# Ramp, turns and hand-over of a fused linear attention and top-1 expert kernel in a new order, and two steps of the first expert's second products over all its columns

## The chip, the cores and the metric

One core of one Trainium2 chip runs one program. The metric is the time of one execution on the device in microseconds, median of three runs. TensorE multiplies, VectorE and GpSimd (POOL in the profile) work element by element, ScalarE evaluates functions and copies, SyncE (SP) issues DMAs. Each engine works through its own instructions in order and waits for the others at semaphores.

## The reference

```
f = sigmoid(f_logit)                         # q, k, v, f_logit: [4, 8, 768, 48]
for t in range(768):                         # per batch and head
    state = f[t, :, None] * state + outer(k[t], v[t])
    y[t] = q[t] @ state
x = y.transpose(0, 2, 1, 3).reshape(3072, 384)
logits = x @ w_gate                          # 8 experts
e = argmax(logits, 1); gate = softmax(logits)[e]
out = gate * sigmoid(x @ w_output_gate)[e] * (relu(x @ w1[e]) @ w2[e])   # w1 384x1024, w2 1024x384
```

Everything is float32. The expert products are made from three matmuls of fp32r pieces each: high by high, low by high, high by low.

## The kernel before, in words

**Attention.** The sequence is cut in chunks of 128 positions, six per batch, 24 in all; a step t is one chunk of one batch, all 8 heads. Within a chunk the gates are turned into running products: ScalarE writes f (L214) into a PSUM bank, VectorE scans it twice, p (L219) and its inverse i (L226), POOL multiplies q by p (L234) and k by i (L231), in place. TensorE then makes the scores a_ps (`qk`, L256), a mask is put on them (half by POOL after a copy, L261 and L262, half by VectorE, `at`, L265), k is transposed (`kn_tr`, L275), and y of the chunk is the sum of a product with the state (`out_state`, L319) and one with the masked scores (`out_at`, L327), in two PSUM banks, two_ps and one_ps. The state is renewed from a product (L292) and two VectorE instructions (L306, L307; one, L304, for the first chunk of a batch). ScalarE copies y out of both banks (`evac_y`, L341), TensorE transposes it and multiplies it by the gate weights (`x_tr`, L350), VectorE finds each token's expert (`route`, L404 to L410) and its slot by a rank product (L433, L435, L441, L443), and POOL scatters the rows by an indirect DMA to a buffer sorted by expert (L369).

**What sets the order.** Nothing is scheduled: the order in which `attention` calls the steps is the order of each engine's instructions. The steps are pipelined: f is made two steps ahead, the scores and y of the previous step stand in one turn of the loop, y is transposed a step later. The first steps fill this pipeline (the ramp, steps 0 to 2). A change of batch, at steps 6, 12 and 18, is called a turn here: there y's sum starts without a state. At the last step, 23, `hand_over` takes the place of the loop's end: it mixes the last two chunks with the start of the experts.

**Experts.** They come in order of their number of tokens, with 448, 432, 416, 400, 400, 384, 368 and 368 columns. F = 1024 is cut in 8 blocks f. `mm1` (L862) makes 9 matmuls per f into h_ps, ScalarE's relu gives the high part (`hh`, L866), VectorE the low one (`hl`, L867); `mm2` (L882, and L896 for later experts) adds 9 matmuls per f to y_ps. Weights are split likewise, the high part on ScalarE (L695), the low part on VectorE or POOL (L696, `w1l`, `w2l`). The first expert starts while the last tokens are still being scattered: its first 224 columns (EARLY) go through mm1 for all f (`mm1_early`) and through mm2 for the first AHEAD = 8 of them; then the late columns are fetched (`x_late`, L812 and L819), and they go through mm1 and mm2. VectorE finds the other tokens' lists in between (`find_order`, L943 to L960).

Of the kernel before, what the change touches and what calls it, by code (L numbers as in the profile page):

```python
# [8 lines left out]
F32 = mybir.dt.float32  # L9
F32R = mybir.dt.float32r  # L10
# [23 lines left out]
HARD = 64  # L34
T_TOP = 16
T_END = 20
AHEAD = 8
KC = DM // 128
KF = F // 128
BIG = 8192  # L40
# [25 lines left out]
def make_consts(nc, k, pool, prep, ps, ends):  # L66

    k.warm = pool.tile([128, 512], BF16, name="warm")
    nc.vector.memset(k.warm, 0.0)
    warm_up(nc, k, ps, WARM)  # L70
    k.act = pool.tile([128, 1], F32, name="act")
    nc.scalar.activation(out=k.act, in_=k.warm[:, 0:1], func=AF.Sigmoid)

    for a in ends:
        nc.vector.memset(a, 0.0)

    k.start_p = [prep.tile([128, NP, C], F32, name=f"start_p{i}", bufs=1) for i in range(2)]
    for t in k.start_p:
        nc.vector.memset(t, PFLOOR)

    k.start_i = [prep.tile([128, NP, C], F32, name=f"start_i{i}", bufs=1) for i in range(2)]
    for t in k.start_i:
        nc.vector.memset(t, 0.0)
    k.ident = pool.tile([128, 128], F32, name="ident")
    make_identity(nc, k.ident)

    k.mask = pool.tile([128, NP, C], F32, name="mask")
    nc.gpsimd.memset(k.mask, 1.0)
    nc.gpsimd.affine_select(out=k.mask, in_=k.mask, pattern=[[0, NP], [1, C]], compare_op=ALU.is_ge,
                            fill=0.0, base=0, channel_multiplier=-1)  # L90


# [42 lines left out]
def attention(ctx, tc, nc, k, kpool, rt, q01, k01, f01, q23, k23, f23, v, wg, xs_dram, r, ex):  # L135
# [61 lines left out]
    def prep(ti):  # L197
        b, c = order[ti]
        i, sl, z = b % 2, slice(c * C, (c + 1) * C), ti % 2
        flat = lambda a: a.rearrange("p g t -> p (g t)")  # L200
        eng = nc.vector if ti == last else nc.gpsimd
        kcuts = [slice(0, 2), slice(2, NP)] if ti in (1, 2) else [slice(0, NP)]
        d = {}

        def s():

            nc.scalar.activation(out=k.start_p[z][:, :, 0:1], in_=f_t[i][:, :, c * C:c * C + 1], func=AF.Sigmoid)  # L207
            d["p"] = pf.tile([128, NP, C], F32, name="p", bufs=3)
            nc.scalar.copy(out=d["p"][:, 0, 0:1], in_=k.start_p[z][:, 0, 0:1])

        def f():

            d["f"] = {1: f_y, 2: f_o, 4: f_m}.get(ti, f_ps)
            nc.scalar.activation(out=d["f"][:, :, 0:C - 1], in_=f_t[i][:, :, c * C + 1:c * C + C], func=AF.Sigmoid)  # L214

        def scan_p():

            n, sp = NP * C, flat(k.start_p[z])
            nc.vector.tensor_tensor_scan(out=flat(d["p"])[:, 1:n], data0=flat(d["f"])[:, 0:n - 1], data1=sp[:, 1:n],  # L219
                                         initial=sp[:, 0:1], op0=ALU.mult, op1=ALU.max)  # L220

        def scan_i():

            nc.vector.reciprocal(out=k.start_i[z][:, :, C - 1:C], in_=d["p"][:, :, C - 1:C])
            d["i"] = pf.tile([128, NP, C], F32, name="i", bufs=3)
            nc.vector.tensor_tensor_scan(out=flat(d["i"])[:, ::-1], data0=flat(d["f"])[:, ::-1],  # L226
                                         data1=flat(k.start_i[z])[:, ::-1], initial=0.0, op0=ALU.mult, op1=ALU.max)

        def mul_k():
            for h in kcuts:  # L230
                eng.tensor_tensor(out=k_t[i][:, h, sl], in0=k_t[i][:, h, sl], in1=d["i"][:, h], op=ALU.mult)  # L231

# [11 lines left out]
    def hot(t):  # L244
        return 0 <= t < len(order)
# [200 lines left out]
    def hand_over():  # L446
        even, odd = (0, 1, 4, 5), (2, 3, 6, 7)
        run_pq()
        evac_y(last - 1, (0,))
        state_upd(last - 1)  # L450
        evac_y(last - 1, (1,))
        ex.x_early_turn()
        y_at(last)
        out_at(last, even, True)
        out_at(last, odd, True)
        scatter(4)
        x_tr(last - 1)
        ex.x_early()
        for heads in (even, odd):
            out_state(last, heads, False)  # L460
        evac_x(last - 1)
        evac_y(last)
        ex.split(1, 0, 1)
        ex.mm1_early(0)
        x_tr(last)
        evac_x(last)
        route(len(RG) - 1, last - 1, 2)
        drain()
        ex.split(1, 0, 2)
        ex.mm1_early(1)  # L470
        ex.split(1, 0, 3, nc.gpsimd)
        ex.mm1_early(2)
        run_pq()
        scatter(len(sq))
        ex.tokens_in(0, FIRST // TS, NT)
        ex.meta_in(0)

# [18 lines left out]

    done = [set() for _ in order]
    f_y, f_m = pairs(two), pairs(misc)
    f_o = pairs(one)
    make_consts(nc, k, kpool, pf, psA.tile([128, 2, 512], F32, name="kx")[:, 0, :],  # L500
                [a[:, :, C - 1:C] for a in (f_ps, f_y, f_o, f_m)])
    for st in states:
        nc.gpsimd.memset(st, 0.0)
    for g in range(2):
# [19 lines left out]
    for t in range(last + 1):  # L524
# [26 lines left out]
        fill(more)  # L551
        kn_tr(t)
        if t == 0:
            warm_up(nc, k, misc, 3)
        if t == last:
            run_pq(ready)
        if hot(t - 2):
            x_tr(t - 2)
        evac_kn(t)
# [5 lines left out]
        if t == last:  # L565
            route(*ends[t - 2])
            drain()
        fill(more)
        if T_END <= t < last:
            fill(8)  # L570
# [4 lines left out]
            psX.append(ctx.enter_context(tc.tile_pool(name="psX", bufs=1, space=PSUM)))  # L575
        if hot(t - 1):
            out_y(t - 1)
            if order[t - 1][1] < NCH - 1 and t < last and not ready:
                evac_y(t - 1, (0,))
                halved.append(t - 1)  # L580
            state(t - 1)
# [1 line left out]
            hand_over()  # L583
            break
        run_pq(ready)
        if t >= T_END:
            pre(t + 2, "mul_k")
        if t >= T_SCAT:
            scatter(1 if t < T_END else 2)
# [18 lines left out]
        if t + 1 == last:  # L608
            drain()
            assert ex.xq  # L610
            ex.split(1, 0, 0)
    for f in range(3, KF):
        ex.mm1_early(f)
        if f == 3:
# [6 lines left out]
class Experts:  # L621
# [4 lines left out]
    def __init__(self, tc, nc, k, r, raw, right, w1, w2, xs_dram, out, kp):  # L626
        self.tc, self.nc, self.k, self.r, self.raw, self.right, self.kp = tc, nc, k, r, raw, right, kp
        self.w1, self.w2, self.xs, self.out = w1, w2, xs_dram.rearrange("(e n) w -> e n w", e=E), out

        self.first = kp.tile([128, SLOTS // BL, QW], F32, name="first_x")  # L630
        self.apart, self.number, self.meta, self.put_out = [], {}, {}, []
        self.cleared = {HELD // TS: []}
        self.wr, self.whl, self.todo, self.gq = {}, {}, [], []
        self.xq, self.xt, self.hs, self.ysb = {}, {}, {}, {}

    def open_early(self):
# [47 lines left out]
            self.wr[2, s, i] = t  # L684

    def split(self, m, s, i, eng=None):
        to = of = lambda a: a.rearrange("p a b -> p (a b)")
        if m == 2 and s < TURNED:
            to = lambda a: a.rearrange("p a b -> p (a b)").rearrange("p (c x i) -> p x c i", c=KC, i=BL)
            of = lambda a: a.rearrange("p a (q c i) -> p (a q) c i", c=KC, i=BL)  # L690
        t = self.wr.pop((m, s, i))
        shape = [128, KC, 256] if m == 1 else [128, 2, DM]
        hi = self.wp.tile(shape, F32R, name=f"w{m}h")
        lo = self.wp.tile(shape, F32R, name=f"w{m}l")
        self.nc.scalar.copy(out=to(hi), in_=of(t))  # L695
        (eng or self.nc.vector).tensor_tensor(out=to(lo), in0=of(t), in1=to(hi.bitcast(F32)), op=ALU.subtract)  # L696
        self.whl[m, s, i] = (hi, lo)


    def rows(self, s):  # L700
        return [(j, min(TS, CAPS[s] - j * TS)) for j in range(NT) if CAPS[s] > j * TS]
# [149 lines left out]
    def mm1(self, s, f, early=False):  # L851
# [6 lines left out]
        for c in range(KC):  # L858
            cs = slice((f % 2) * 128, (f % 2) * 128 + 128)
            xh, xl = self.xt[x, c]  # L860
            for a, b in ((wh, xh), (wh, xl), (wl, xh)):
                nc.tensor.matmul(ps[:, 0:n], a[:, c, cs], b, start=(i == 0), stop=(i == 3 * KC - 1))  # L862
                i += 1
        pool, width = (self.ha, EARLY) if early else (self.hp, WIDE)
        hi, lo = (pool.tile([128, width], F32R, name=m)[:, 0:n] for m in ("hh", "hl"))
        nc.scalar.activation(out=hi, in_=ps[:, 0:n], func=AF.Relu)  # L866
        nc.vector.scalar_tensor_tensor(out=lo, in0=ps[:, 0:n], scalar=0.0, in1=hi.bitcast(F32), op0=ALU.max,  # L867
                                       op1=ALU.subtract)
        self.hs.setdefault((s, f), []).append((hi, lo))
# [450 lines left out]
```

## Time and profile before

| | us |
|---|---|
| median of 3 runs (338.42 to 339.17) | 338.83 |
| the profiled execution | 339.06 |
| its span | 337.3 |
| TensorE matmuls busy | 327.0 |
| VectorE, ScalarE, POOL busy | 244.2, 197.8, 198.5 |

The span is the time from the first to the last instruction. The granted TensorE clock is full in the whole span. A row of a timeline is one instruction or several alike, with its start, the time it took, engine and line, operation, and in brackets the idle time before it on its engine and what ended that. PEld is the weight load that precedes each matmul; its idle times show TensorE's pauses most clearly. In the chain of waits each step follows from what released the next.

### The profile page before, as it was taken

What the parts mean: (1) busy time and instruction counts of PE and PEld (TensorE: products, weight loads), DVE (VectorE), ACT (ScalarE), POOL (GpSimd) and SP (SyncE); (2) the same over time, 40 slices, a digit from 0 to 9 for tenths busy, and PEclk for the clock granted to TensorE, in tenths of its full rate; (3) what the DMA queues carried; (4) which work ended last, traced back from release to release, by engine and by line L of the source; (5) the groups of instructions that cost most, each with busy time, mean ns of one, the idle gap of its engine ahead of it and who ended that gap; (6) DMA issues with size and microseconds to landing.
All of it is one profiled execution on the core that took longest, in us unless ns stands there. A gap on an engine that the chain in (4) does not pass through costs nothing.

```text
span 337.3 us, 8735 instructions
## 1 busy us (share of the span) xinstructions
PE 327.0 (97%) x3117; PEld 309.2 (92%) x3118; DVE 244.2 (72%) x492; ACT 197.8 (59%) x495; POOL 198.5 (59%) x239
## 2 busy tenths in 40 slices
PE   8799999999999999999999999999999999999992
PEld 3698898988898799999999999999999999999992
DVE  5999989898998687596776776767767665765700
ACT  4677776776676573445743763772773675654510
POOL 7997798999998643010684376286376188522021
PEclk9999999999999999999999999999999999999999
DMA  7999999999934964989795395484495495621001
GB/s 247 336 350 348 310 235 256 253 285 256 260 115 157 272 264 83 250 243 230 224 243 121 107 266 126 145 233 143 140 224 156 137 209 169 208 76 41 0 25 46
DMA packets 75924, 65.68 MB, mean 195 GB/s; under 512 B 28495, under 2 KB 73332, under 8 KB 75872
## 3 DMA queue, kind: packets, MB, share of 16 engines
q1 hardware_dynamic: 71616, 55.39, 62.8%
q0 software_dynamic: 4256, 9.65, 8.7%
q8 instruction: 26, 0.43, 0.6%
q14 instruction: 26, 0.21, 0.2%
HBM read 53.73 MB, written 11.58 MB: 194 GB/s over the span
## 4 chain that ended last, share of the span: by engine, by line
PE 76%; DVE 9%; DMA 5%; issue 4%; POOL 2%; ACT 2%; POOLq 0%; ACTq 0%; DVEq 0%
PE h_ps L862 30%; PE y_ps L882 21%; PE y_ps L896 9%; DMA q_t<-in_q 4%; PE a_ps L256 4%; PE kx L350 4%; DVE i L226 3%; PE two_ps L327 2%; DVE p L219 2%; PE one_ps L327 2%; PE two_ps L319 2%; PE one_ps L292 2%; DVE at L265 2%; DMA f_t<-in_f 1%; PE kx L275 1%
## 5 line engine op out<-in xcount | busy, mean ns | idle before, releaser
L917 POOL DMA_INDIRECT out<-yr,dst x67 | 74.6, 1113 | 55.2 <-ACT yr L916 33.4
L862 PE MATMUL h_ps<-xh,w1h 128*128 128x400 f32 (+5 forms) x192 | 63.7, 332 | 0.0
L862 PE MATMUL h_ps<-xh,w1l 128*128 128x400 f32 (+5 forms) x192 | 63.7, 332 | 0.0
L862 PE MATMUL h_ps<-xl,w1h 128*128 128x400 f32 (+5 forms) x192 | 63.7, 332 | 0.0
L867 DVE SCALAR_TENSOR_TENSOR hl<-h_ps,hh 128x224 fp32r<-128x224 f32 (+5 forms) x72 | 37.9, 527 | 33.6 <-ACT hh L866 33.4
L866 ACT ACTIVATE hh<-h_ps 128x224 fp32r<-128x224 f32 (+5 forms) x72 | 33.8, 469 | 40.4 <-PE h_ps L862 40.2
L882 PE MATMUL y_ps<-hh,w2h 128*128 128x224 f32 (+3 forms) x144 | 46.6, 323 | 0.0
L882 PE MATMUL y_ps<-hh,w2l 128*128 128x224 f32 (+3 forms) x144 | 46.5, 323 | 0.0
L882 PE MATMUL y_ps<-hl,w2h 128*128 128x224 f32 (+3 forms) x144 | 46.5, 323 | 0.0
L696 DVE TENSOR_TENSOR w1l<-w1r,w1h 128x768 fp32r<-128x768 f32 x31 | 29.5, 956 | 15.3 <-ACT w1h L695 15.1
L862 PEld LDWEIGHTS h_ps<-xh,w1h 128*128 128x128 f32 x192 | 36.1, 188 | 0.2
L862 PEld LDWEIGHTS h_ps<-xl,w1h 128*128 128x128 f32 x192 | 36.1, 188 | 0.2
L862 PEld LDWEIGHTS h_ps<-xh,w1l 128*128 128x128 f32 x192 | 36.1, 188 | 0.2
L234 POOL TENSOR_TENSOR q_t<-q_t,p 128x512 f32<-128x512 f32 x24 | 30.6, 1273 | 2.0 <-DVE p L219 1.7
L231 POOL TENSOR_TENSOR k_t<-k_t,i 128x512 f32<-128x512 f32 (+1 forms) x25 | 29.7, 1193 | 2.6 <-DVE i L226 1.3
L696 DVE TENSOR_TENSOR w2l<-w2r,w2h 128x768 fp32r<-128x768 f32 x31 | 29.7, 958 | 1.7 <-ACT w2h L695 0.9
L219 DVE TENSOR_TENSOR_SCAN p<-f_ps,start_p 128x511 f32<-128x511 f32 x21 | 26.7, 1273 | 4.2 <-ACT start_p L207 2.2
L256 PE MATMUL a_ps<-q_t,k_t 64*128 64x128 f32 x384 | 28.2, 285 | 1.2 <-POOL k_t L231 1.1
L818 ACT CAST xh<-xr 128x400 fp32r<-128x400 f32 (+5 forms) x24 | 11.9, 505 | 28.7 <-DVE xr L812 25.2
L369 POOL DMA_INDIRECT xs_dram<-xn,slot x24 | 24.2, 1009 | 7.6 <-issue 4.6
L882 PEld LDWEIGHTS y_ps<-hh,w2h 128*128 128x128 f32 x144 | 27.3, 189 | 0.2
L882 PEld LDWEIGHTS y_ps<-hl,w2h 128*128 128x128 f32 x144 | 27.2, 189 | 0.2
(174 smaller groups left out, 768.7 us busy)
## 6 DMA issues: line engine op xcount, KB each, us to landing
w1r<-in_w SPq DMA_DIRECT2D x32, 384.0 KB, 5.3
w2r<-in_w SPq DMA_DIRECT2D x32, 384.0 KB, 3.5
v_t<-in_v SPq DMA_DIRECT2D x24, 256.0 KB, 8.0
f_t<-in_f SPq DMA_DIRECT2D x6, 512.0 KB, 8.9
q_t<-in_q SPq DMA_DIRECT2D x6, 512.0 KB, 7.1
k_t<-in_k SPq DMA_DIRECT2D x6, 512.0 KB, 5.9
f_t<-in_f SPq DMA_DIRECT2D x12, 192.0 KB, 8.1
k_t<-in_k SPq DMA_DIRECT2D x12, 192.0 KB, 8.2
```

Source lines behind the costliest of these rows:

```text
L219: nc.vector.tensor_tensor_scan(out=flat(d["p"])[:, 1:n], data0=flat(d["f"])[:, 0:n - 1], data1=sp[:, 1:n], initial=sp[:, 0:1], op0=ALU.mul ...
L231: eng.tensor_tensor(out=k_t[i][:, h, sl], in0=k_t[i][:, h, sl], in1=d["i"][:, h], op=ALU.mult)
L234: nc.gpsimd.tensor_tensor(out=q_t[i][:, :, sl], in0=q_t[i][:, :, sl], in1=d["p"], op=ALU.mult)
L256: nc.tensor.matmul(aps[t][par][:, g, :], k_t[b % 2][r, g, sl], q_t[b % 2][r, g, sl], start=(g == 0), stop=(g == NP - 1))
L369: i = nc.gpsimd.indirect_dma_start(out=xs_dram, out_offset=bass.IndirectOffsetOnAxis(ap=r.slot[:, t:t + 1], axis=0), in_=xn[t // 4][:, t % ...
L696: (eng or self.nc.vector).tensor_tensor(out=to(lo), in0=of(t), in1=to(hi.bitcast(F32)), op=ALU.subtract)
L862: nc.tensor.matmul(ps[:, 0:n], a[:, c, cs], b, start=(i == 0), stop=(i == 3 * KC - 1))
L866: nc.scalar.activation(out=hi, in_=ps[:, 0:n], func=AF.Relu)
L867: nc.vector.scalar_tensor_tensor(out=lo, in0=ps[:, 0:n], scalar=0.0, in1=hi.bitcast(F32), op0=ALU.max, op1=ALU.subtract)
L882: self.nc.tensor.matmul(self.ys[d][:, c0:c0 + n], a, b, start=(f == 0 and i == 0 and part == 0), stop=(f == KF - 1 and i == 2), skip_group ...
L896: nc.tensor.matmul(ps[0:n, 0:DM], a, b[:, f % 2, :], start=(i == 0), stop=(i == 3 * KF - 1))
L917: self.other_rows(self.nc.gpsimd.indirect_dma_start(out=self.out.rearrange("n (q w) -> (n q) w", q=NQ), out_offset=bass.IndirectOffsetOnAx ...
```

## The change

- **Ramp.** The f of chunk 2 goes to the bank `misc` instead of `one`. Two warm-up matmuls into `one` at step 0 instead of three into `misc`. The second half (heads 4 to 7) of `mul_k` of chunk 2 goes from POOL to VectorE. The mask has 128 columns instead of 512 and is read by broadcast.
- **Turns.** At steps 6, 12 and 18 the copy of the first half of y follows right behind `out_y`, so ahead of the next f on ScalarE, and `mul_k` of step t+2 comes ahead of the scatter on POOL.
- **Hand-over.** `split` is cut in `split_hi` and `split_lo`. The low part of w1 block 0 comes behind the slots of step 21 on VectorE; the transposes of the early columns come ahead of the rank of step 22; the copy of the first half of y(22) right behind `out_y`; `mul_k(23)` behind the state of step 20; the low parts of w1 blocks 2 (used from f=4) and 3 behind the slots of step 23, both on VectorE, where block 3 was on POOL ahead of the last two scatters.
- **First expert.** AHEAD = 6: mm2 of the early columns takes f = 0 to 5 ahead of the late columns; for f = 6 and 7 both parts of the hidden values lie in one tile (`fh`, `fl`) and mm2 takes all 448 columns at once.

```diff
-AHEAD = 8
+AHEAD = 6
@@ make_consts
-    k.mask = pool.tile([128, NP, C], F32, name="mask")
+    k.mask = pool.tile([128, C], F32, name="mask")
@@ prep
-            d["f"] = {1: f_y, 2: f_o, 4: f_m}.get(ti, f_ps)
+            d["f"] = {1: f_y, 2: f_m, 4: f_m}.get(ti, f_ps)
...
-                eng.tensor_tensor(out=k_t[i][:, h, sl], in0=k_t[i][:, h, sl], in1=d["i"][:, h], op=ALU.mult)
+                on = nc.vector if ti == 2 and h.start else eng
+                on.tensor_tensor(out=k_t[i][:, h, sl], in0=k_t[i][:, h, sl], in1=d["i"][:, h], op=ALU.mult)
@@ mask
-        nc.vector.tensor_tensor(out=at[t][:, par], in0=aps[t][par], in1=k.mask, op=ALU.mult)
+        nc.vector.tensor_tensor(out=at[t][:, par], in0=aps[t][par], in1=k.mask.unsqueeze(1).broadcast_to([128, NP, C]),
+                                op=ALU.mult)
@@ hand_over
-        evac_y(last - 1, (0,))
+        evac_y(last - 1, (1,))
         state_upd(last - 1)
-        evac_y(last - 1, (1,))
-        ex.x_early_turn()
...
-        ex.split(1, 0, 2)
+        ex.split_hi(1, 0, 2)
         ex.mm1_early(1)
-        ex.split(1, 0, 3, nc.gpsimd)
+        ex.split_hi(1, 0, 3)
         ex.mm1_early(2)
         run_pq()
         scatter(len(sq))
+        ex.split_lo(1, 0, 2)
+        ex.split_lo(1, 0, 3)
@@ attention, the loop over t
+        if t == last:
+            ex.split_hi(1, 0, 0)
...
         if t == 0:
-            warm_up(nc, k, misc, 3)
+            warm_up(nc, k, one, 2)
         if t == last:
             run_pq(ready)
+            ex.split_lo(1, 0, 0)
...
             drain()
+            ex.x_early_turn()
...
             out_y(t - 1)
-            if order[t - 1][1] < NCH - 1 and t < last and not ready:
+            if t == last or not ready:
                 evac_y(t - 1, (0,))
...
-        if t >= T_END:
+        if T_END <= t < last - 2 or order[t][1] == 0:
             pre(t + 2, "mul_k")
...
         if t + 1 == last:
             drain()
             assert ex.xq
-            ex.split(1, 0, 0)
@@ mm1
-        pool, width = (self.ha, EARLY) if early else (self.hp, WIDE)
-        hi, lo = (pool.tile([128, width], F32R, name=m)[:, 0:n] for m in ("hh", "hl"))
+        if s == 0 and f >= AHEAD:
+            if early:
+                self.whole[f] = [self.ha.tile([128, WIDE], F32R, name=m, bufs=KF - AHEAD) for m in ("fh", "fl")]
+            hi, lo = (t[:, 0:n] if early else t[:, EARLY:EARLY + n] for t in self.whole[f])
...
+        if s == 0 and f >= AHEAD:
+            self.hs[s, f] = [tuple(t[:, 0:CAPS[0]] for t in self.whole[f])]
```

VectorE's order in the ramp, before (i and p are scans of a chunk's f, which is read from the PSUM bank named first; `at` is the masked half of the scores):

```order
L219 SCALAR_TENSOR_TENSOR p<-one_ps,start_p_183 128x511
L224 RECIPROCAL start_i_187<-p 128x4
L226 SCALAR_TENSOR_TENSOR i<-one_ps,start_i_187 128x512
L265 TENSOR_TENSOR at<-a_ps,mask 128x512
L219 SCALAR_TENSOR_TENSOR p<-f_ps,start_p_184 128x511
L224 RECIPROCAL start_i_188<-p 128x4
L226 SCALAR_TENSOR_TENSOR i<-f_ps,start_i_188 128x512
L304 TENSOR_TENSOR state_106<-one_ps,pend 128x4x48
```

VectorE at the same place of the changed kernel:

```order
L219 SCALAR_TENSOR_TENSOR p<-misc,start_p_182 128x511
L224 RECIPROCAL start_i_186<-p 128x4
L226 SCALAR_TENSOR_TENSOR i<-misc,start_i_186 128x512
L232 TENSOR_TENSOR k_t_100<-k_t_100,i 128x2x128
L266 TENSOR_TENSOR at<-a_ps,mask 128x512
L219 SCALAR_TENSOR_TENSOR p<-f_ps,start_p_183 128x511
L224 RECIPROCAL start_i_187<-p 128x4
L226 SCALAR_TENSOR_TENSOR i<-f_ps,start_i_187 128x512
L306 TENSOR_TENSOR state_106<-one_ps,pend 128x4x48
```

The scan of chunk 2 reads misc instead of one_ps, and half of k_t stands between it and the mask of step 1, ahead of the first state.

VectorE's order at the hand-over, from the routing of step 21 on, before (rk and slot are the slots of a pair of steps, w1l the low part of a block of w1, misc and state the two halves of a state's renewal):

```order
L404 TENSOR_REDUCE ohb<-ohb 128x8
L696 TENSOR_TENSOR w1l<-w1r,w1h 128x768
L306 TENSOR_TENSOR misc<-one_ps,state_106 128x192
L307 TENSOR_TENSOR state_107<-misc,pend 128x4x48
L265 TENSOR_TENSOR at<-a_ps,mask 128x512
L441 TENSOR_TENSOR rk<-two_ps,ohb 128x16
L443 TENSOR_REDUCE slot<-rk 128x2
```

VectorE at the same place of the changed kernel:

```order
L406 TENSOR_REDUCE ohb<-ohb 128x8
L308 TENSOR_TENSOR misc<-one_ps,state_106 128x192
L309 TENSOR_TENSOR state_107<-misc,pend 128x4x48
L266 TENSOR_TENSOR at<-a_ps,mask 128x512
L443 TENSOR_TENSOR rk<-two_ps,ohb 128x16
L445 TENSOR_REDUCE slot<-rk 128x2
L710 TENSOR_TENSOR w1l<-w1r,w1h 128x768
```

The low part of the first block of w1 now stands behind the state, the mask and the slots.

VectorE's order at the first expert's start, before (hl is the low part of the hidden values of one f, from f = 0):

```order
L696 TENSOR_TENSOR w1l<-w1r,w1h 128x768
L867 SCALAR_TENSOR_TENSOR hl<-h_ps,hh 128x224
L406 TENSOR_REDUCE xn<-lgp 128x2x16
L409 TENSOR_REDUCE misc<-xn 128x2
L410 TENSOR_TENSOR ohb<-xn,misc 128x16
L404 TENSOR_REDUCE ohb<-ohb 128x8
L696 TENSOR_TENSOR w1l<-w1r,w1h 128x768
L867 SCALAR_TENSOR_TENSOR hl<-h_ps,hh 128x224 x2
L441 TENSOR_TENSOR rk<-two_ps,ohb 128x16
L443 TENSOR_REDUCE slot<-rk 128x2
L867 SCALAR_TENSOR_TENSOR hl<-h_ps,hh 128x224
```

VectorE at the same place of the changed kernel:

```order
L710 TENSOR_TENSOR w1l<-w1r,w1h 128x768
L884 SCALAR_TENSOR_TENSOR hl<-h_ps,hh 128x224
L408 TENSOR_REDUCE xn<-lgp 128x2x16
L411 TENSOR_REDUCE misc<-xn 128x2
L412 TENSOR_TENSOR ohb<-xn,misc 128x16
L406 TENSOR_REDUCE ohb<-ohb 128x8
L884 SCALAR_TENSOR_TENSOR hl<-h_ps,hh 128x224 x2
L443 TENSOR_TENSOR rk<-two_ps,ohb 128x16
L445 TENSOR_REDUCE slot<-rk 128x2
L710 TENSOR_TENSOR w1l<-w1r,w1h 128x768 x2
L884 SCALAR_TENSOR_TENSOR hl<-h_ps,hh 128x224
```

The second w1l of these rows (block 2) moved behind rk and slot of step 23, and block 3 joined it from POOL.

## Rows read from the trace of the kernel before

**Rows 1.** Page, section 1: busy us, share of the span, instructions, by engine

```profile
PE 327.0 (97%) x3117; PEld 309.2 (92%) x3118; DVE 244.2 (72%) x492; ACT 197.8 (59%) x495; POOL 198.5 (59%) x239
```

**Rows 2.** Timeline, weight loads: start, us, engine, line, operation, [idle before <-releaser]

```profile
14.49 0.20 PEld L327 LDWEIGHTS one_ps<-at,v_t 128*64 128x64 f32 x4 [0.78 <-DVE i L226]
...
15.74 0.97 PEld L256 LDWEIGHTS a_ps<-q_t,k_t 64*128 64x128 f32 x16
...
18.15 0.14 PEld L319 LDWEIGHTS two_ps<-q_t,state 64*64 64x64 f32 x2
...
39.06 0.97 PEld L350 LDWEIGHTS kx<-turn,xt 128*128 128x128 f32 x8 [0.33 <-ACT xt L341]
...
67.83 1.04 PEld L256 LDWEIGHTS a_ps<-q_t,k_t 64*128 64x128 f32 x16 [0.22 <-POOL k_t L231]
...
106.17 0.14 PEld L319 LDWEIGHTS two_ps<-q_t,state 64*64 64x64 f32 x2 [0.29 <-DVE state L307]
...
111.24 0.14 PEld L319 LDWEIGHTS two_ps<-q_t,state 64*64 64x64 f32 x2 [0.87 <-DVE rk L441]
...
114.28 0.42 PEld L327 LDWEIGHTS two_ps<-at,v_t 128*64 128x64 f32 x8 [0.38 <-ACT xt L341]
```

**Rows 3.** Chain of waits from the hand-over: start, us, engine and line

```profile
122.14 4.12 PE h_ps L862 x36
126.25 8.04 PE y_ps L882 x72
134.29 8.04 PE h_ps L862 x72
...
150.37 14.11 PE h_ps L862 x72
...
178.70 13.44 PE h_ps L862 x72
```

**Rows 4.** Timeline, VectorE, ramp: scan of chunk 2 and first state

```profile
13.21 1.22 DVE L226 TENSOR_TENSOR_SCAN i<-one_ps,start_i 128x512 f32<-128x512 f32 x1
...
17.67 0.33 DVE L304 TENSOR_TENSOR state<-one_ps,pend 128x192 f32<-128x192 f32 x1
```

**Rows 5.** Timeline, POOL, ramp: both halves of k_t of chunk 2

```profile
14.52 1.42 POOL L231 TENSOR_TENSOR k_t<-k_t,i 128x256 f32<-128x256 f32 x2
```

**Rows 6.** Timeline, VectorE, hand-over: k_t of step 23 and w1l

```profile
104.38 1.07 DVE L231 TENSOR_TENSOR k_t<-k_t,i 128x512 f32<-128x512 f32 x1
...
108.89 0.96 DVE L696 TENSOR_TENSOR w1l<-w1r,w1h 128x768 fp32r<-128x768 f32 x1 [1.27 <-ACT w1h L695]
```

**Rows 7.** Timeline, VectorE, token list: two products over 128x64

```profile
126.78 1.87 DVE L952 TENSOR_TENSOR cube<-okey 128x64 f32<-128x64 f32 x1
...
129.37 0.22 DVE L955 TENSOR_TENSOR cube<-perm,num 128x64 f32<-128x64 f32 x1
```

**Rows 8.** Timeline, POOL: a scatter at turn 2, a subtraction near the token list

```profile
65.44 1.01 POOL L369 DMA_INDIRECT xs_dram<-xn,slot  x1 [0.17 <-issue]
...
126.45 2.12 POOL L696 TENSOR_TENSOR w2l<-w2r,w2h 128x768 fp32r<-128x768 f32 x1 [1.04 <-ACT w2h L695]
```

**Rows 9.** Timeline, ScalarE, turn 1: the copy that x_tr waits for

```profile
38.65 0.36 ACT L341 COPY xt<-two_ps 128x256 f32<-128x256 f32 x1
```

**Rows 10.** Timeline, VectorE, hand-over: rank, transposes, last slot

```profile
113.59 0.17 DVE L441 TENSOR_TENSOR rk<-two_ps,ohb 128x16 f32<-128x16 f32 x1 [1.15 <-PE two_ps L435]
...
114.55 1.00 DVE L812 STREAM_TRANSPOSE xar<-first_x 128x224 f32<-128x224 f32 x3
...
121.95 0.17 DVE L443 TENSOR_REDUCE slot<-rk 128x2 int32<-128x16 f32 x1
```

**Rows 11.** Timeline, VectorE: end of the token list and the late columns

```profile
131.25 0.22 DVE L960 TENSOR_REDUCE tokens<-cube 128x8 f32<-128x64 f32 x1
131.85 1.00 DVE L812 STREAM_TRANSPOSE xr<-first_x 128x224 f32<-128x224 f32 x3 [0.38 <-issue]
132.77 0.97 DVE L819 TENSOR_TENSOR xl<-xr,xh 128x224 fp32r<-128x224 f32 x3
```

More of the change, by code (lines that the diff above doesn't have):

```diff
@@ L85, in make_consts @@
     make_identity(nc, k.ident)
-    k.mask = pool.tile([128, NP, C], F32, name="mask")
+    k.mask = pool.tile([128, C], F32, name="mask")
     nc.gpsimd.memset(k.mask, 1.0)
-    nc.gpsimd.affine_select(out=k.mask, in_=k.mask, pattern=[[0, NP], [1, C]], compare_op=ALU.is_ge,
+    nc.gpsimd.affine_select(out=k.mask, in_=k.mask, pattern=[[1, C]], compare_op=ALU.is_ge,
                             fill=0.0, base=0, channel_multiplier=-1)
@@ L498, in attention @@
     f_y, f_m = pairs(two), pairs(misc)
-    f_o = pairs(one)
     make_consts(nc, k, kpool, pf, psA.tile([128, 2, 512], F32, name="kx")[:, 0, :],
-                [a[:, :, C - 1:C] for a in (f_ps, f_y, f_o, f_m)])
+                [a[:, :, C - 1:C] for a in (f_ps, f_y, f_m)])
     for st in states:
@@ L632, in __init__ @@
         self.cleared = {HELD // TS: []}
-        self.wr, self.whl, self.todo, self.gq = {}, {}, [], []
+        self.wr, self.whl, self.rest, self.whole, self.todo, self.gq = {}, {}, {}, {}, [], []
         self.xq, self.xt, self.hs, self.ysb = {}, {}, {}, {}
@@ L686, in split, with split_hi @@
     def split(self, m, s, i, eng=None):
+        self.split_hi(m, s, i)
+        self.split_lo(m, s, i, eng)
+    def split_hi(self, m, s, i):
         to = of = lambda a: a.rearrange("p a b -> p (a b)")
@@ L695, in split, with split_lo @@
         self.nc.scalar.copy(out=to(hi), in_=of(t))
+        self.whl[m, s, i] = (hi, lo)
+        self.rest[m, s, i] = (t, to, of)
+    def split_lo(self, m, s, i, eng=None):
+        t, to, of = self.rest.pop((m, s, i))
+        hi, lo = self.whl[m, s, i]
         (eng or self.nc.vector).tensor_tensor(out=to(lo), in0=of(t), in1=to(hi.bitcast(F32)), op=ALU.subtract)
-        self.whl[m, s, i] = (hi, lo)
     def rows(self, s):
@@ L863, in mm1 @@
                 i += 1
-        pool, width = (self.ha, EARLY) if early else (self.hp, WIDE)
-        hi, lo = (pool.tile([128, width], F32R, name=m)[:, 0:n] for m in ("hh", "hl"))
+        if s == 0 and f >= AHEAD:
+            if early:
+                self.whole[f] = [self.ha.tile([128, WIDE], F32R, name=m, bufs=KF - AHEAD) for m in ("fh", "fl")]
+            hi, lo = (t[:, 0:n] if early else t[:, EARLY:EARLY + n] for t in self.whole[f])
+        else:
+            pool, width, bufs = (self.ha, EARLY, AHEAD) if early else (self.hp, WIDE, 9)
+            hi, lo = (pool.tile([128, width], F32R, name=m, bufs=bufs)[:, 0:n] for m in ("hh", "hl"))
         nc.scalar.activation(out=hi, in_=ps[:, 0:n], func=AF.Relu)
@@ L868, in mm1 @@
                                        op1=ALU.subtract)
-        self.hs.setdefault((s, f), []).append((hi, lo))
+        if s == 0 and f >= AHEAD:
+            self.hs[s, f] = [tuple(t[:, 0:CAPS[0]] for t in self.whole[f])]
+        else:
+            self.hs.setdefault((s, f), []).append((hi, lo))
     def mm1_early(self, f):
```

## The prediction

> **What bounds the kernel now.** I read the page first: TensorE is busy for 97% of the span [rows 1], so outside its pauses the time is a queue of matrix products, and another engine matters only where it makes TensorE wait. The second view is the timeline of the weight loads, which run just ahead of the matmuls: the bracket behind a row is the idle time before it and what ended it. The six pauses of the ramp, the turns and the hand-over are the rows at 14.49, 39.06, 67.83, 106.17, 111.24 and 114.28, of 0.78, 0.33, 0.22, 0.29, 0.87 and 0.38 us, 2.87 in all [rows 2]. The third view is the chain of waits behind the hand-over: runs of matmuls end to end [rows 3], so a microsecond lost or won ahead of 122.14 is still there at the end, unless a later stage waits. The fourth is what the releasing engines do at the six places.
>
> The profiled execution took 339.06 us, 337.3 of it span. The sum is made against that; the median of the three runs, 338.83, is 0.23 lower, and the forecast is moved by as much. Times of day below are before's.
>
> **The ramp, first pause.** y(0) goes to two banks, and one of them was held by the f of chunk 2 until its scan ended at 13.21 + 1.22 = 14.43 [rows 4]. With that f in another bank TensorE goes on at once: of 0.78 all but the usual 0.1 is won there, and it comes to a_ps(2) at 15.74 - 0.68 = 15.06 [rows 2]. It finds POOL's half of k_t(2) nearly done: from 14.52, 1.42/2 = 0.71, to 15.23 [rows 5]. But VectorE now has the other half, ahead of the mask, in a stretch that ends with state(0) at 17.67 + 0.33 = 18.00 [rows 4], and the load that needs state(0) stands at 18.15 [rows 2]: 0.15 later. Nearly every added microsecond D on VectorE comes through. D has no row of its own. The whole product on VectorE took 1.07, a half of it 0.53; a subtraction of 768 columns took 0.96, so 256 columns 0.32, the lower end [rows 6]; waiting for POOL's half and then running, 0.71 + 0.53 = 1.24, is the upper end. I take 0.53, the same operation on the same engine. The load goes from 18.15 to 18.00 + 0.53 + 0.07 = 18.60, with the 0.07 that I take for a released wait: **+0.45** (+0.24 to +1.16). Behind it TensorE runs full steps, so it stays. The pause is won, and a larger wait put behind it. The warm-up matmul and memset that go and the smaller mask lie where TensorE waits for POOL's first k_t anyway, and cost or give nothing; if that cover were gone it would be a tenth. The mask read by broadcast has as many elements, and I price the read at zero, plus or minus 0.1.
>
> The Trainium skill's page "SBUF — State Buffer", section "Who interferes with whom", says that a VectorE instruction with two SBUF inputs contends with a GpSimd instruction that reads SBUF, and that whichever issues first has the port for its whole length. That speaks against sharing k_t(2) out over both engines. The trace agrees at the token list: 1.87 us for the cube at 126.78 [rows 7] beside a POOL subtraction of 2.12 begun at 126.45 [rows 8], against 0.22 for a cube of the same 128x64 at 129.37. By that rule nothing is lost if VectorE issues first; what it makes of the other order is the slower rival below.
>
> **The turns.** At 39.06 x_tr waited for the copy of two_ps at 38.65 [rows 9], which stood behind an f that waits for a scan. Now the copy goes ahead of f. Of 0.33 - 0.1 = 0.23 about half stays won, since in the next step the copy stands behind f again, and that f hangs on the same scans: -0.12. At 67.83 k_t came 0.22 late, behind a scatter of 1.01 on POOL at 65.44 [rows 8]; with k_t ahead of it that goes: -0.18. The scatter is later by one k_t, and nobody on TensorE waits for it. The third turn has no pause. Together **-0.30** (-0.45 to -0.05).
>
> **The hand-over up to the first expert.** The load at 106.17 waited for a state that stood behind k_t(23) on VectorE, 1.07 at 104.38 [rows 2, 6]; that product moves behind: 0.29 less what is usual, **-0.18**. At 111.24 VectorE was late because w1l (0.96, after 1.27 of waiting for ScalarE) stood ahead of state, mask and rank [rows 2, 6]; it now stands behind the slots, and TensorE goes straight on from x_tr: 0.87 - 0.11, **-0.76**. At 114.28 two_ps waited for a copy that waited for the rank at 113.59 [rows 2, 10]. The copy is early now, but the rank stands behind the three transposes (1.00) that were at 114.55 [rows 10]; half of 0.28 is won, **-0.14** (0 to -0.28). The first product of the first expert so starts 1.08 earlier, counted without ramp and turns.
>
> **New wait one, w1l for f=4.** Before, this subtraction stood between the results of f=0 and f=1. Now both remaining w1l (2 x 0.96) come behind the slots of step 23 on VectorE. The slot row stood at 121.95 [rows 10]; 1.08 earlier and with nothing large ahead of it, it ends near 120.8, since it follows the results of f=2, and w1l is there near 121.7. The third matmul of f=4 needs it, at about 121.87 with the latency of 0.15 seen at 18.15; it was at 122.14 + 0.22 = 122.36 [rows 3]. So f=4 is 0.49 earlier, not 1.08: **+0.59** (0 to +0.9), with a pause of some 0.6 in front of it. Behind the two w1l on VectorE stand the lo of f=3, the counts and the token list.
>
> **New wait two, late columns.** The second products ahead of the late columns are 54 matmuls, not 72, of 8.04/72 = 0.1117 each [rows 3]: TensorE comes to the late columns at 134.29 - 0.49 - 18 x 0.1117 = 131.79, and wants the first xl with its second matmul, 131.90. Their inputs hang on VectorE's queue: the token list ends at 131.25 + 0.22 = 131.47, then three transposes (0.92 from start to the next start) and the first subtraction (a third of 0.97, and latency, 0.35) [rows 11]. With the list 0.49 earlier and no pause of its own behind it: 130.98 + 0.92 + 0.35 = 132.25, and 0.15 to the matmul, 132.40: **+0.51** (0 to +0.9). Before, this was hidden under the 72 matmuls.
>
> **Joined columns.** 36 matmuls of 224 columns, 4.02, become 18 of 448. No row has 448: 416 take 13.44/72 = 0.187, 432 take 14.11/72 = 0.196 [rows 3]; by the slope from 224 to 416, 0.00039 a column, 448 take 0.199, by the two widest 0.205. I take 0.200, so 3.60: **-0.42** (-0.33 to -0.44).
>
> **Sum.** +0.45 - 0.30 - 0.18 - 0.76 - 0.14 + 0.59 + 0.51 - 0.42 = -0.25. 339.06 - 0.25 = 338.81 profiled, about **338.6** against the median shown. What goes in six places comes back in three: ahead of state(0)'s load, at f=4, and at the late columns.
>
> **Rivals.** *It does all it says:* no new wait takes the place of a pause. Each pause leaves 0.07 of ordinary gap: 2.87 - 0.42 = 2.45, and 0.42 of joining: 338.83 - 2.87 = 336.0. For it: VectorE had 1.27 and 1.15 idle at the hand-over [rows 6, 10], so its queue could catch up. Against it: in the ramp only 0.15 was to spare.
>
> *The ramp's new wait comes, the hand-over's two don't:* 338.6 - 0.59 - 0.51 = 337.5. For it: half a microsecond less on VectorE is enough for either. Against it: two subtractions now stand in one place ahead of the list.
>
> *Slower, the shared port in the ramp:* POOL's half issues first, VectorE's waits 0.71 for it and then takes 0.53. state(0) is 1.24 later and its load at 19.31: +1.16 for +0.45, so 339.3; with POOL's price for the half, 0.71 for 0.53, 339.5. It decides from the point where VectorE's half starts after 15.2. For it: the cube's 1.87 [rows 7]. Against it: both halves are released by the same scan, VectorE ran that scan itself, and POOL's product began 0.09 behind its end [rows 4, 5].
>
> **How the numbers follow.** A measurement of this kernel can tell a change of about 0.2%, 0.68 us, from none: faster is below 338.15, slower above 339.51. The forecast gets 0.48, with its own range of 338.0 to 339.3 by the bounds of D and of the two waits; 336.0 gets 0.12, 337.5 gets 0.22, the port 0.18. Faster: 0.12 + 0.22 and a little of the forecast's own, 0.36. Slower: most of the port's cases, since the two hand-over waits can be 0.3 longer as well, 0.15. Same: 0.49. The range is 336.9 to 339.6: below lies most of the first rival, above the last one's tail.
>
> **What would show it.** Right: no idle at y(0), and one of about 0.5 ahead of the first load of state(0), ended by VectorE; no 0.87 at the load of step 23; a wait of about 0.6 in f=4 for w1l, and one at the first late matmuls for xl; 18 matmuls of 448 at 0.2 each. Wrong: a half on VectorE of 0.3 or of 1.2; no wait at f=4, then the slots were early and the time is nearer 337.5; or a stage behind 150 that gives back what was won.

## The result, and the profile after

The change takes 341.26 us, median of 7 runs (340.53 to 343.37), against 338.83 us of 7 runs before (338.07 to 339.88): a ratio of 1.0074 with a 95% interval of 1.0054 to 1.0093. It is slower, by 2.4 us, where no measurable change was forecast. The profiled execution took 341.71 us with a span of 340.0.

The page's first section, as in [rows 1]: TensorE is busy for as long as before in a longer span, with 18 matmuls fewer, since 18 joined ones stand for 36.

```profile
PE 327.0 (96%) x3099; PEld 308.8 (91%) x3099; DVE 247.2 (73%) x493; ACT 197.7 (58%) x495; POOL 195.5 (58%) x237
```

The weight loads at the places of [rows 2], and three new ones:

```profile
13.50 0.25 PEld L329 LDWEIGHTS one_ps<-at,v_t 128*64 128x64 f32 x4
...
15.76 1.00 PEld L257 LDWEIGHTS a_ps<-q_t,k_t 64*128 64x128 f32 x16 [1.00 <-POOL k_t L232]
...
18.72 0.14 PEld L321 LDWEIGHTS two_ps<-q_t,state 64*64 64x64 f32 x2 [0.63 <-DVE state L306]
...
39.37 0.74 PEld L352 LDWEIGHTS kx<-turn,xt 128*128 128x128 f32 x6
...
68.06 0.97 PEld L257 LDWEIGHTS a_ps<-q_t,k_t 64*128 64x128 f32 x16
...
105.73 0.14 PEld L321 LDWEIGHTS two_ps<-q_t,state 64*64 64x64 f32 x2
...
110.11 0.14 PEld L321 LDWEIGHTS two_ps<-q_t,state 64*64 64x64 f32 x2
...
114.48 0.42 PEld L329 LDWEIGHTS two_ps<-at,v_t 128*64 128x64 f32 x8 [1.62 <-DVE rk L443]
...
123.13 0.19 PEld L874 LDWEIGHTS h_ps<-xah,w1l 128*128 128x128 f32 x1 [0.77 <-DVE w1l L710]
...
133.65 0.19 PEld L874 LDWEIGHTS h_ps<-xh,w1h 128*128 128x128 f32 x1 [0.61 <-ACT xh L830]
134.07 0.19 PEld L874 LDWEIGHTS h_ps<-xl,w1h 128*128 128x128 f32 x1 [0.24 <-DVE xl L831]
```

The pause at y(0) is gone (13.50), as are those of 0.33 and 0.22 at the first two turns (39.37, 68.06), 0.29 (105.73) and 0.87 (110.11). New are 1.00 ahead of the scores of chunk 2, 0.63 ahead of state(0), 1.62 at 114.48 where there was 0.38, 0.77 in f=4, and 0.61 and 0.24 at the late columns. That is 4.87 us of idle, counting the 1.62 whole. The 1.00 takes back what was won at y(0): the scores of chunk 2 start at 15.76, for 15.74 before.

VectorE at the places of [rows 4, 6, 10 and 11]:

```profile
14.66 0.43 DVE L232 TENSOR_TENSOR k_t<-k_t,i 128x256 f32<-128x256 f32 x1 [0.27 <-DMA k_t<-in_k]
...
18.34 0.33 DVE L306 TENSOR_TENSOR state<-one_ps,pend 128x192 f32<-128x192 f32 x1
...
104.86 2.34 DVE L232 TENSOR_TENSOR k_t<-k_t,i 128x512 f32<-128x512 f32 x1
...
110.36 1.16 DVE L710 TENSOR_TENSOR w1l<-w1r,w1h 128x768 fp32r<-128x768 f32 x1
...
113.37 1.00 DVE L824 STREAM_TRANSPOSE xar<-first_x 128x224 f32<-128x224 f32 x3 [0.93 <-DMA first_x<-xs_dram]
114.29 0.14 DVE L443 TENSOR_TENSOR rk<-two_ps,ohb 128x16 f32<-128x16 f32 x1
...
122.04 0.17 DVE L445 TENSOR_REDUCE slot<-rk 128x2 int32<-128x16 f32 x1
122.13 1.85 DVE L710 TENSOR_TENSOR w1l<-w1r,w1h 128x768 fp32r<-128x768 f32 x2
...
132.13 0.22 DVE L980 TENSOR_REDUCE tokens<-cube 128x8 f32<-128x64 f32 x1
...
133.65 0.97 DVE L831 TENSOR_TENSOR xl<-xr,xh 128x224 fp32r<-128x224 f32 x3
```

At 113.37 the bracket names a transfer: the three transposes of the early columns waited for first_x to arrive, and the rank at 114.29 (it is that of chunks 20 and 21) stands behind them. The rank reads two_ps, the bank that TensorE's product at 114.48 writes, so TensorE waits for it. In [rows 10] the rank came first, at 113.59, and the transposes found their data. POOL's half of k_t(2), for [rows 5]:

```profile
14.70 0.97 POOL L232 TENSOR_TENSOR k_t<-k_t,i 128x256 f32<-128x256 f32 x1 [0.42 <-DMA k_t<-in_k]
```

The half on VectorE took 0.43 and POOL's 0.97, where it was 0.71. Both waited for the load of k_t first. The chain behind the hand-over, for [rows 3]:

```profile
134.07 8.19 PE h_ps L874 x71
142.26 9.76 PE y_ps L902 x72
152.02 14.09 PE h_ps L874 x72
...
180.34 13.56 PE h_ps L874 x72
...
334.22 0.95 POOL out L948
```

The second products of the late step are 54 x 0.1117 = 6.03 and 18 joined ones, so 9.76 - 6.03 = 3.73, 0.207 each. Where the time went, by the shift of the same instruction (after minus before; each step's forecast beside its increment):

| up to | shift | increment | forecast |
|---|---|---|---|
| load of state(0), 18.15 to 18.72 | +0.57 | +0.57 | +0.45 |
| scores after both turns, chain 72.45 to 72.61 | +0.16 | -0.41 | -0.30 |
| load of step 22, 106.17 to 105.73 | -0.44 | -0.60 | -0.18 |
| load of step 23, 111.24 to 110.11 | -1.13 | -0.69 | -0.76 |
| two_ps at the last step, 114.28 to 114.48 | +0.20 | **+1.33** | **-0.14** |
| last POOL issue, 332.32 to 334.22 | +1.90 | +1.70 | +0.68 |

The increment of -0.60 at the load of step 22 isn't all the change's. In the kernel before, TensorE paused in the middle of eight like products with one state, and the profile names no engine that it waited for:

```profile
88.72 0.13 PEld L319 LDWEIGHTS one_ps<-q_t,state 64*64 64x64 f32 x1 [0.32 <-issue]
```

The change's profile has no such pause. The products behind it, 89.29 before and 89.01 after, are at a shift of -0.28, so 0.44 was won by then and 0.16 behind it, near the 0.18 that was forecast for moving k_t(23). The pause stands at the same load in eight of the fourteen profiles, with 0.30 to 1.03, and in six not at all (the change, e1, e4, c1, c2, c3). One profile for each kernel can't tell whether the order brings it or one execution has it and the next not.

The last line of the table holds w1l for f=4, the late columns and the joined columns, +0.59 + 0.51 - 0.42 = 0.68. It also holds 0.24 that the change doesn't explain: the two stages of 416 columns took 13.56 instead of 13.44 each, as they did in e1, e2, e3 and others, but not in e4 and c1. Behind the last issue the span runs 4.83 us more, for 4.03 before; this tail was 3.8 to 4.9 in the experiments' profiles and holds no work of an engine that could name a cause.

### The profile page after: what moved, and what is told of

The parts are those of the page before. It is cut to its first block, busy times and chain, and to the rows that moved or that the text cites. A ratio compares the mean times of both kernels' runs of the same rounds, so it can differ in the third digit from the quotient of the medians.

```text
span 340.0 us, 8694 instructions
## 1 busy us (share of the span) xinstructions
PE 327.0 (96%) x3099; PEld 308.8 (91%) x3099; DVE 247.2 (73%) x493; ACT 197.7 (58%) x495; POOL 195.5 (58%) x237
## 4 chain that ended last, share of the span: by engine, by line
PE 80%; DMA 5%; DVE 4%; issue 4%; POOL 2%; SPq 1%; ACT 1%; POOLq 0%; DVEq 0%; ACTq 0%
PE h_ps L874 30%; PE y_ps L902 19%; PE y_ps L916 9%; PE a_ps L257 6%; PE kx L352 6%; PE two_ps L329 3%; DMA k_t<-in_k 3%; PE two_ps L321 2%; PE one_ps L329 2%; PE one_ps L294 2%; DMA first_x<-xs_dram 1%; PE kx L277 1%; DMA xs_dram<-xn,slot 1%; DVE w2l L710 1%; SPq L191 1%
## 5 line engine op out<-in xcount | busy, mean ns | idle before, releaser
L884 DVE SCALAR_TENSOR_TENSOR hl<-h_ps,hh 128x400 fp32r<-128x400 f32 (+5 forms) x68 | 36.4, 536 | 32.4 <-ACT hh L883 32.2
L883 ACT ACTIVATE hh<-h_ps 128x400 fp32r<-128x400 f32 (+5 forms) x68 | 32.4, 476 | 40.8 <-PE h_ps L874 40.6
L902 PE MATMUL y_ps<-hh,w2h 128*128 128x400 f32 (+3 forms) x132 | 43.4, 329 | 0.0
L902 PE MATMUL y_ps<-hl,w2h 128*128 128x400 f32 (+3 forms) x132 | 43.3, 328 | 0.0
L902 PE MATMUL y_ps<-hh,w2l 128*128 128x400 f32 (+3 forms) x132 | 43.3, 328 | 0.0
L710 DVE TENSOR_TENSOR w1l<-w1r,w1h 128x768 fp32r<-128x768 f32 x32 | 30.6, 963 | 14.6 <-ACT w1h L703 13.6
L371 POOL DMA_INDIRECT xs_dram<-xn,slot x24 | 25.1, 1044 | 12.7 <-issue 5.4
L257 PEld LDWEIGHTS a_ps<-q_t,k_t 64*128 64x128 f32 x384 | 23.5, 187 | 4.4 <-POOL k_t L232 3.0
L703 ACT CAST w2h<-w2r 128x768 fp32r<-128x768 f32 x32 | 26.4, 826 | 0.0
```

The lines of the kernel that those rows point to most:

```text
L257: nc.tensor.matmul(aps[t][par][:, g, :], k_t[b % 2][r, g, sl], q_t[b % 2][r, g, sl], start=(g == 0), stop=(g == NP - 1))
L902: self.nc.tensor.matmul(self.ys[d][:, c0:c0 + n], a, b, start=(f == 0 and i == 0 and part == 0), stop=(f == KF - 1 and i == 2), skip_group ...
```

## The experiments

Ratios are to the kernel before on the same chip, with their 95% intervals; each has 6 or more runs. The experiments ran on several chips, where the kernel before took 338.63 to 339.63, so a difference of medians between two groups holds the difference of their chips too.

**Each new wait taken away alone.** e1 moves one call:

```diff
             drain()
-            ex.x_early_turn()
...
         state_upd(last - 1)
+        ex.x_early_turn()
```

> The change, with the three transposes of the early columns back behind the state of step 22, so behind the rank and slots of step 22 on VectorE. Theory (new waits): the pause of 1.62 us ahead of two_ps at step 23 comes from the rank queued behind transposes that wait for a transfer (landed near 113.3). It falls to 0.3 or less, the first product of the first expert starts 1.2 earlier (from 116.82 to about 115.6), and the time is 341.26 - 1.2 = 340.0. Rival (swallowed later): the waits for w1l in f=4 and for the late columns hang on VectorE and grow by as much; the pause goes, the time stays within 0.3 of 341.26.

339.50 us, 1.0029 (1.0008 to 1.0051): 1.76 less by the medians and 1.5 by the ratios, where 1.2 was expected; the interval doesn't meet the change's. VectorE at that place:

```profile
112.19 0.17 DVE L443 TENSOR_TENSOR rk<-two_ps,ohb 128x16 f32<-128x16 f32 x1 [0.18 <-PE two_ps L437]
...
113.15 0.99 DVE L824 STREAM_TRANSPOSE xar<-first_x 128x224 f32<-128x224 f32 x3
```

The rank now runs at 112.19, and the transposes behind it at 113.15, with no idle time before them. The pause went, and the first product of the first expert starts at 114.79 in the chain, for 116.82. From the load of state(0), which was 0.36 earlier in this execution, that is 96.43 for 98.10, so 1.67 less. The rival is out: the waits in f=4 and at the late columns kept their 0.77, 0.61 and 0.24 to a hundredth.

e2 puts back the low parts of w1 blocks 2 and 3:

```diff
-        ex.split_hi(1, 0, 2)
+        ex.split(1, 0, 2)
         ex.mm1_early(1)
-        ex.split_hi(1, 0, 3)
+        ex.split(1, 0, 3, nc.gpsimd)
...
-        ex.split_lo(1, 0, 2)
-        ex.split_lo(1, 0, 3)
```

> The change, with the low parts of w1 blocks 2 and 3 where they stood before (block 2 on VectorE ahead of the results of f=1, block 3 on POOL). Theory (new waits): the idle of 0.77 at the third weight load of f=4 goes, and the token list ends 0.9 earlier, so the wait at the late columns does not grow: 341.26 - 0.7 = 340.6. Rival (swallowed later): the late columns wait 0.7 longer, 341.2.

340.48 us, 1.0063 (1.0039 to 1.0087): 0.78 less by the medians. The 0.77 went; the late columns wait as they did (0.61 and 0.24 in the change), since the list on VectorE moved with TensorE:

```profile
133.04 0.19 PEld L872 LDWEIGHTS h_ps<-xh,w1h 128*128 128x128 f32 x1 [0.66 <-ACT xh L828]
133.47 0.19 PEld L872 LDWEIGHTS h_ps<-xl,w1h 128*128 128x128 f32 x1 [0.24 <-DVE xl L829]
```

e3 is `AHEAD = 8` in the change, so that no columns are joined.

> The change, with AHEAD = 8, so all second products of the early columns ahead of the late ones, and no joined columns. Theory (new waits): the waits of 0.61 and 0.24 at the late columns go, and the 0.31 won by 18 matmuls of 448 columns is lost: 341.26 - 0.85 + 0.31 = 340.7. Rival (the joined columns are a gain by themselves and the late columns wait anyway): 341.5.

340.50 us, 1.0065 (1.0039 to 1.0090): 0.76 less by the medians, 0.54 expected. No load at the late columns waits.

e4 is `on = eng` for both halves of k_t(2), so both are on POOL.

> The change, with both halves of k_t of chunk 2 on POOL. Theory (VectorE is the bound of the ramp): the load of state(0) goes back from 18.72 to about 18.2 and the time falls by 0.5, to 340.75. Rival (the ramp waits for its loads): k_t of chunk 2 lands near 14.6 whichever engine multiplies it, POOL then needs 1.42 for it, the scores of chunk 2 start near 16.0 for 15.76, and the time stays at 341.2 or rises to 341.5.

340.76 us, 1.0068 (1.0050 to 1.0087): 0.50 less by the medians, as the theory said. By the ratios the intervals of e2, e3 and e4 overlap the change's, so for these three the traces decide:

```profile
15.22 0.52 PEld L257 LDWEIGHTS a_ps<-q_t,k_t 64*128 64x128 f32 x8 [0.37 <-POOL k_t L232]
...
17.97 0.14 PEld L321 LDWEIGHTS two_ps<-q_t,state 64*64 64x64 f32 x2 [0.22 <-DVE state L306]
```

The load of state(0) is at 17.97, for 18.72 (18.36 to 18.48 in e1, e2 and e3, whose loads landed 0.3 earlier). It still waits 0.22 for VectorE. With k_t on POOL the ramp, from the first scores (9.82 before, 9.73 here) to this load, takes 8.24 for 8.33. The pause of 0.78 at y(0) was worth 0.1.

**All four back.** c1 has the four edits together.

> The change with all four pieces put back: k_t of chunk 2 on POOL, the transposes behind the rank, the low parts of w1 blocks 2 and 3 in their old places, AHEAD = 8. What is left of the change: f in misc, the turns, k_t(23) behind the state, the first w1l behind the slots, the early copy of y(22). Theory (the four waits are separate): the four gains measured one by one add up, 341.26 - 1.76 - 0.78 - 0.76 - 0.50 = 337.5, so 1.3 faster than before. Rival (they are one wait seen at four places, since all hang on VectorE's queue): no more than the largest of them and a little, 339.0 or above.

337.59 us, 0.9969 (0.9950 to 0.9987). The medians add up: 3.80 in four parts, 3.67 together. By the ratios the parts sum to 2.4 and c1 to 3.6; each difference of two ratios has an uncertainty of some 1.0, and so this doesn't contradict. The rival of one wait seen at four places, with 339.0 or more, is out: the waits are separate in the main, and what is left of the change is a gain of 1.0 on that chip.

c2 and c3 are c1 with `AHEAD = 7` and `AHEAD = 6`.

> As c1, with AHEAD = 7, so that one f of two is joined: 9 matmuls of 448 columns, and 1.0 us of early second products more ahead of the late columns than in the change. Theory: the late columns' wait of 0.85 is covered by that microsecond, and half of the join's gain of 0.31 is left: 0.15 less than c1, 337.3. Rival (the late columns come too late anyway): 0.3 more than c1.

> As c1, with AHEAD = 6 as in the change. Theory: the wait of 0.61 and 0.24 at the late columns is there as in the change, the join gives 0.31: 0.54 more than c1, 338.0. Rival (with the list earlier on VectorE the late columns are ready): 0.3 less than c1.

c2: 337.25 us, 0.9951 (0.9933 to 0.9968); c3: 338.31 us, 0.9989 (0.9971 to 1.0007). In c3 the late columns wait longer than in the change, since TensorE comes to them 3.13 sooner (129.91 for 133.04) and the first xl only 2.84 (its product at 131.23 for 134.07):

```profile
130.81 0.19 PEld L872 LDWEIGHTS h_ps<-xh,w1h 128*128 128x128 f32 x1 [0.90 <-ACT xh L828]
131.23 0.19 PEld L872 LDWEIGHTS h_ps<-xl,w1h 128*128 128x128 f32 x1 [0.24 <-DVE xl L829]
```

In c2 the chain runs through them without a wait, and the late second products take 8.87, 63 x 0.1117 + 9 x 0.204:

```profile
124.35 7.04 PE y_ps L900 x63
131.39 8.05 PE h_ps L872 x72
139.44 8.87 PE y_ps L900 x72
...
330.55 0.95 POOL out L946
```

So one joined step is free and two cost 1.1 us of waiting for 0.3 of gain. c2 is the fastest of all kernels here, by its ratio 1.7 us (1.1 to 2.3) faster than the kernel before, though it isn't separated from c1.

**The turns.** p1 is the kernel before with the turns' two edits (`if t < last and not ready`, `or order[t][1] == 0`).

> The kernel before with the turns alone: at steps 6, 12 and 18 the copy of two_ps right behind out_y and k_t ahead of the scatter. Theory: the pauses of 0.33 at 39.06 and 0.22 at 67.83 go, and 0.40 is won, 338.4. Rival (the prediction's: half of the first comes back a step later): 0.30, 338.5. Nothing won, 338.8, if the gain is swallowed at the hand-over.

338.82 us, 0.9994 (0.9978 to 1.0010): nothing measurable won, the third outcome named, within half a microsecond. The pauses at the turns are gone from the trace, and the one of [rows 2] at 111.24 has grown from 0.87 to 1.25. Counted from the first scores (9.55 for 9.82), p1 is 0.41 ahead at the product with the masked scores before it (106.09 for 106.77) and 0.03 at this load. The three engines there, TensorE, VectorE, POOL:

```profile
110.94 0.14 PEld L319 LDWEIGHTS two_ps<-q_t,state 64*64 64x64 f32 x2 [1.25 <-DVE rk L441]
```

```profile
108.21 1.33 DVE L696 TENSOR_TENSOR w1l<-w1r,w1h 128x768 fp32r<-128x768 f32 x1 [1.49 <-ACT w1h L695]
```

```profile
108.73 1.30 POOL L262 TENSOR_SCALAR_AFFINE_SELECT at<-at 128x512 f32<-128x512 f32 x1
...
110.08 0.62 POOL L262 TENSOR_SCALAR_AFFINE_SELECT at<-at 128x512 f32<-128x512 f32 x1
```

The subtraction of w1, 0.96 in [rows 6], took 1.33, and the POOL instruction that began in it 1.30, where its twin at 110.08 took 0.62. Come earlier by what the turns won, the two met. This was ahead of the rank that step 23 waits for. s3 asks whether the turns pay where that subtraction is out of the way: c1 without them.

> As c1, without the turns: the copy of two_ps and k_t at steps 6, 12 and 18 in the old order. Theory (the turns are worth 0.40, which alone was eaten because the subtraction of w1 at the hand-over met a POOL instruction and took 1.33 for 0.96): 0.4 above c1, 338.0. Rival (they are worth nothing by themselves): 337.6.

337.62 us, 0.9963 (0.9947 to 0.9978): the same as c1. The expected 0.4 didn't show, though with an uncertainty of 0.8 it isn't out either. In c1's trace the scores at 72.01 wait 0.31 for k_t on POOL and the loads of states at 96.24 and 100.98 wait 0.27 and 0.36, none of which s3 has. That the turns cause these waits isn't shown: c2, which has the turns too, has only one of 0.18 at 100.38. And s3's profile has the pause of no named engine (0.30 at 88.25), c1's hasn't. s4 is s3 with `AHEAD = 7`.

> As s3 (the change without the turns and with the four pieces put back), with AHEAD = 7: one f joined. Theory (the turns give nothing on the whole, the joined f gives 0.15 to 0.3 as between c1 and c2): 0.995 of the kernel before, like c2. Rival (the turns pay once the hand-over doesn't eat them, and s3 was as fast as c1 by chance): 0.4 slower than c2, 0.9965 or above.

338.34 us against 339.63 before on that chip, 0.9972 (0.9958 to 0.9986). It lies nearer to the rival, but its interval meets those of c2, c1 and s3: what the turns are worth stays open within half a microsecond.

**The ramp.** s1 is c2 with the second scan of chunk 3 behind the first state; s2 is that with the half of k_t(2) on VectorE.

```diff
-        pre(t + 2, "scan_p", "scan_i")
+        pre(t + 2, "scan_p", *(("scan_i",) if t != 1 else ()))
...
         if t == 2:
+            pre(3, "scan_i")
```

> As c2 (k_t of chunk 2 on POOL, one f joined), with the first state's product ahead of the second scan of chunk 3 on VectorE. Theory (the load of state(0) waits for its place in VectorE's queue): the wait of 0.22 ahead of it goes, 0.2 less than c2, 337.05. Rival (TensorE then waits for the scores of chunk 3, whose scan is 0.33 later): same as c2 or 0.1 more.

> As s1, with the second half of k_t of chunk 2 on VectorE as in the change. Theory (the half cost 0.5 in the change only because state(0) stood behind it and the scan in one queue): within 0.2 of s1, and the load of state(0) starts with no wait of VectorE. Rival (the half costs by itself, by the port it shares with POOL's half): 0.4 or more above s1.

s1: 337.93 us, 0.9965 (0.9952 to 0.9978); s2: 338.01 us, 0.9971 (0.9958 to 0.9983). Neither beats c2. By time s1's 0.2 didn't come, but the comparison isn't clean, since both profiles have the pause of no named engine, 1.03 in s1 and 0.85 in s2, and c2's hasn't. In the traces, from the first scores to the load of state(0), c2 takes 8.24, s1 8.14 and s2 8.19. The two are alike, and in s2 the load of state(0) waits for nothing:

```profile
15.53 1.00 PEld L257 LDWEIGHTS a_ps<-q_t,k_t 64*128 64x128 f32 x16 [0.65 <-POOL k_t L232]
...
17.96 0.14 PEld L321 LDWEIGHTS two_ps<-q_t,state 64*64 64x64 f32 x2
```

So the half on VectorE costs next to nothing by itself. In the change it cost because state(0) stood behind it in a queue that had no gap. The port decided nothing there: VectorE issued first and POOL's half paid (0.97, and 0.71 where both are on POOL) where it had time: state(0) came later still.

## Why the prediction was wrong

**The step that failed is the last of the hand-over,** "the rank stands behind the three transposes (1.00) that were at 114.55 [rows 10]; half of 0.28 is won, **-0.14** (0 to -0.28)". It priced the transposes by their own length and not by what they wait for. In [rows 10] they have no bracket because they stood late, behind the state, when their data was there. Ahead of the rank they wait 0.93 for first_x, and rank, slots, two_ps and everything behind wait with them: +1.33 for -0.14, so 1.47 off. Of this 0.93 is the transfer. The rest is the transposes' own length, which was priced too low as well: without the transfer 1.62 - 0.93 = 0.69 of idle would be left at this load, where the step left 0.38 - 0.14 = 0.24. e1 gives the loss back: 341.26 - 1.76 = 339.50, at the upper end of the range that was stated (336.9 to 339.6); by its ratio, 1.0029 x 338.83 = 339.8, just above it. Either is about 1 above the forecast of 338.6.

This step makes half of what the forecast of the profiled execution missed, +2.65 for -0.25. The three new waits were short by 0.64, the joined columns by 0.13. The tail behind the last issue (0.80) and the stages of 416 columns (0.24) added to it, and the pause at 88.72 that the change's profile lacks took about 0.4 away; the rest are tenths.

**Right, in place and near in size:** the ramp, where the won pause comes back ahead of state(0) (+0.57, or +0.4 where the loads landed earlier, for +0.45; an idle of 0.63 for about 0.5); w1l for f=4 (idle 0.77 for about 0.6); the late columns (0.85 for 0.51). All three were forecast as waits on VectorE, and the traces of e4, e2 and e3 show each of them shrink or go with its piece. In this profile they were 0.12, 0.18 and 0.34 short, the same way. The ramp's near hit is in part luck. VectorE's half took 0.43 for the 0.53 taken, and 0.27 of waiting for the load of k_t came on top, which the sum doesn't have. And TensorE didn't find POOL's half nearly done: it waited 1.00 for it, where 15.23 - 15.06 = 0.17 was forecast.

**Joined columns:** -0.42 forecast, 4.02 - 3.73 = -0.29 measured. 448 columns take 0.207 here and in e1, and 0.203 in e2, e4 and c3, whose stage takes 9.68 or 9.69; the 0.205 from the two widest rows was nearer than the 0.200 taken.

**The turns:** -0.30 forecast and -0.41 in the trace, but no measurable time of their own (p1, s3). "The third turn has no pause" overlooked the 0.32 at 88.72. The sum took a microsecond won early as still there at the hand-over; p1 shows it eaten at step 23 by a meeting of two instructions.

**The rivals:** "does all it says" and "the hand-over's two don't come" are out. The slower one, the shared port in the ramp, has the right sign and the wrong cause: VectorE's half took 0.43, not 1.24. The port showed elsewhere: k_t(23) on VectorE took 2.34 at 104.86, for 1.07, where nobody waited, and w1l 1.33 in p1, where TensorE did. That the port is the cause is argued from the overlap alone; no run takes it away. For these the rule of the Trainium skill's page "SBUF — State Buffer" ("Who interferes with whom"), that a VectorE instruction with two SBUF inputs and a GpSimd one that reads SBUF contend, agrees with the trace; that the first to issue holds the port whole would make the loser's length alone grow, and in p1 both grew.

Not settled: the 0.24 of the 416-column stages, the tail behind the last issue, 0.8 longer in this profile, and the pause at 88.72. All three vary among the experiments' profiles.

## What to carry to other kernels

An instruction that has no wait in its old place may have one in a new place: before a step is moved forward on an in-order engine, look up when its inputs land, its transfers above all, and who is queued behind it. A pause of the bounding engine is worth its length only if the next thing it needs is ready; here 0.78 us was worth 0.1, since the next input hung on an engine without a gap. Work that is cut to save time (72 products to 54 ahead of the late columns) was also cover, so shorten it only as far as what it covers is early.

## What was not expected of the hardware

One VectorE operation over two SBUF inputs, k_t over 128x512, took 0.98 and 1.07 us in the order before (p1 and [rows 6]) and 2.19 to 2.34 in the change and all kernels made from it, where it lay beside a POOL product of q and p. 448 columns took 0.203 to 0.207 a matmul and 432 took 0.196, where 416 took 0.187 in some profiles and 0.188 in others of the same code for that stage. In the middle of eight like products with one state, near 89, TensorE paused for 0.30 to 1.03 in eight profiles and not at all in six, and no engine is named that it waited for.
